# Last layer in groups of three token tiles, its outer weights converted there

## The chip, the cores and the metric

The kernel runs on one core of a Trainium2 chip. Its time is the device time of one execution in microseconds (us); lower is better. A core has a matrix engine (PE, with its own weight loads, PEld), a vector engine (DVE), a scalar engine (ACT), a general engine (POOL) and a queue engine (SP) that issues the transfers (DMA). Each works through its own list of instructions in order and waits on semaphores of the others. Products are summed in PSUM, eight banks of 2 KB in each of 128 partitions; everything else lies in SBUF.

## The reference

Attention with rotary positions (4 batches, 8 heads, 576 tokens, 64 wide), a soft mixture of 8 experts with 32 slots, and one more layer of 512 to 2048 to 512 with Mish in the middle. The last layer's weights arrive as float64.

```
attn  = softmax(rotate(q) @ rotate(k).T / 8) @ v              # x: 2304 x 512
logits = x @ phi                                              # 2304 x 32
slot_input = softmax(logits, over tokens).T @ x               # 32 x 512
slot_out[e] = relu(slot_input[e] @ w1[e]) @ w2[e]             # 8 experts, 4 slots each
x = softmax(logits, over slots) @ slot_out
h = x @ w_in                                                  # 512 x 2048, float64 given
g = h * tanh(log1p(exp(h)))
out = g @ w_out                                               # 2048 x 512, float64 given
```

## The kernel before

The attention goes through 16 pairs of heads; the table PLAN (lines 27 to 37) interleaves, row by row, the scores of one pair (S, M, E: products, maximum, exponential) with the transposes and products of the pair before (T, K, V, W, X), the rotation of the next, and steps of two side jobs: C is a step of the conversion, F one of the experts' dispatch. A scheduler then moves instructions within each engine's list.

The conversion (lines 492 to 531) turns float64 into float32 by the words of a number, 128 x 512 numbers at a time: load (cv_load, line 186's dma), two scalings on ACT (509, 510), three bit operations on DVE (519 to 521), a product and a sum on POOL (528, 529), and a store to DRAM (531). 32 of them run in the attention: the first 16 make w_in (scr_in), the other 16 make w_out (scr_out). Two raw buffers and two results alternate.

The experts follow: h_ps (line 800) over w1 and so_ps (816) over w2, whose 32 blocks of 1 MB come in through a ring of buffers (fetch, 120, used, 140); NRB = 7 of these are new when the attention has closed. so_ps gives s_t (827), the slots' outputs.

The last layer never forms x: for slices of 256 of the 2048 middle units `inner(j)` (871) multiplies s_t with w_in (m_wp), sums over four partition groups (m_w) and writes wst, and `combine(b)` (858) turns one batch's slot shares into ct, both as a high and a low part, so that wst x ct gives h. A unit is 256 tokens by 256 middle units: `mish(u)` makes hp, g in a high (gh) and a low part (gl); `second(u)`, four units later, adds twelve products (gh with wo_h and wo_l, gl with wo_h) to two sums o_ps. `outer(j)` (850) splits w_out, loaded from scr_out, into wo_h and wo_l. Units go by token tile: 9 tiles, 8 slices in each. PSUM: four banks for hp, two for inner until unit 8, then two more for sums.

## Time and profile before

| | |
|---|---|
| Time, median of 3 runs (lowest to highest) | 687.81 us (687.39 to 689.45) |
| The profiled execution | 682.22 us, its span 680.4 us |
| PE busy | 626.9 us (92%) |
| DVE busy | 399.3 us (59%) |
| ACT busy | 323.9 us (48%) |
| POOL busy | 251.2 us (37%) |
| DMA moved | 115.73 MB, mean 170 GB/s |

Busy shares are means over stages: the attention takes up to about 400 us, the experts up to about 440, the last layer the rest. A matrix engine that is shown as busy is not at its peak, since its ends are modelled. The chain that ended last is followed back from the last instruction, at each step to what released it. In the rows further down an engine's idle time stands with what ended it.

### The profile page before, as it was taken

What the parts mean: (1) busy time and instruction counts of PE and PEld (TensorE: products, weight loads), DVE (VectorE), ACT (ScalarE), POOL (GpSimd) and SP (SyncE); (2) the same over time, 40 slices, a digit from 0 to 9 for tenths busy, and PEclk for the clock granted to TensorE, in tenths of its full rate; (3) what the DMA queues carried; (4) which work ended last, traced back from release to release, by engine and by line L of the source; (5) the groups of instructions that cost most, each with busy time, mean ns of one, the idle gap of its engine ahead of it and who ended that gap; (6) DMA issues with size and microseconds to landing.
All of it is one profiled execution on the core that took longest, in us unless ns stands there. A gap on an engine that the chain in (4) does not pass through costs nothing.

```text
span 680.4 us, 11169 instructions
## 1 busy us (share of the span) xinstructions
PE 626.9 (92%) x4002; PEld 461.8 (68%) x4002; DVE 399.3 (59%) x819; ACT 323.9 (48%) x738; POOL 251.2 (37%) x287
## 2 busy tenths in 40 slices
PE   1698889989999989999999988989999999999997
PEld 1565566767667766776777662356888888888885
DVE  6678767896768877776866540066743343434330
ACT  3656756775767667766765510054412221221220
POOL 6668758866868675786330010000000000000000
PEclk9899989999999979999999999999999999999999
DMA  9777698989688975875577697990000110100111
GB/s 266 178 183 197 179 259 226 254 255 264 167 262 256 291 210 206 244 214 157 185 220 214 233 384 286 349 375 1 32 1 31 32 32 0 32 33 0 32 31 32
DMA packets 63064, 115.73 MB, mean 170 GB/s; under 512 B 13216, under 2 KB 25632, under 8 KB 62496
## 3 DMA queue, kind: packets, MB, share of 16 engines
q1 hardware_dynamic: 63008, 115.01, 55.8%
q8 instruction: 32, 0.52, 0.3%
q14 instruction: 24, 0.20, 0.1%
HBM read 73.40 MB, written 13.11 MB: 127 GB/s over the span
## 4 chain that ended last, share of the span: by engine, by line
PE 66%; DMA 10%; DVE 9%; ACT 6%; SPq 4%; issue 3%; POOL 1%; ACTq 0%; DVEq 0%; POOLq 0%
PE o_ps L923 29%; PE m_av L427 8%; PE t L372 5%; DMA w<-in_moe_w_in_dram 5%; PE s L331 4%; DMA qk_st<-partl 3%; PE s L333 3%; PE hp L899 3%; SPq L315 2%; PE h_ps L800 2%; PE so_ps L816 2%; DVE nmax L359 2%; ACT P L365 2%; DMA w<-in_moe_w_out_dram 2%; PE s L351 1%
## 5 line engine op out<-in xcount | busy, mean ns | idle before, releaser
L359 DVE TENSOR_REDUCE nmax<-s 128x1 f32<-128x576 f32 x144 | 107.9, 751 | 51.3 <-PE s L333 32.8
L365 ACT ACTIVATE P<-s,nmax 128x576 f32<-128x576 f32 x144 | 107.0, 744 | 21.4 <-DVE nmax L359 20.4
L923 PE MATMUL o_ps<-wo_l,gh 128*128 128x512 f32 x288 | 113.5, 395 | 0.0
L923 PE MATMUL o_ps<-wo_h,gh 128*128 128x512 f32 x288 | 111.8, 393 | 0.5 <-ACT wo_h L854 0.4
L923 PE MATMUL o_ps<-wo_h,gl 128*128 128x512 f32 x288 | 112.1, 390 | 0.0
L905 ACT ACTIVATE gg<-hp 128x512 f32<-128x512 f32 x72 | 43.1, 600 | 129.1 <-PE hp L899 110.7
L331 PE MATMUL s<-qk_st 128*128 128x288 f32 x256 | 86.5, 352 | 16.2 <-ACT P L365 6.3
L906 DVE CAST gh<-gg 128x512 fp32r<-128x512 f32 x72 | 30.6, 426 | 104.7 <-ACT gg L905 104.6
L372 PE MATMUL t<-cs,P 128*128 128x128 f32 x512 | 80.8, 286 | 8.9 <-DVE partl L271 5.9
L372 PEld LDWEIGHTS t<-cs,P 128*128 128x128 f32 x512 | 62.5, 146 | 20.2 <-issue 11.0
L331 PEld LDWEIGHTS s<-qk_st 128*128 128x128 f32 x256 | 50.0, 195 | 38.2 <-ACT P L365 13.2
L408 ACT COPY PT<-t 128x512 f32<-128x512 f32 x93 | 53.8, 585 | 43.8 <-PE t L372 42.8
L333 PE MATMUL s<-k_st,qk_st 128*128 128x288 f32 x256 | 74.2, 303 | 0.0
L427 PE MATMUL m_av<-PT,w 128*64 128x320 f32 (+1 forms) x384 | 70.1, 420 | 0.2 <-ACT PT L408 0.2
L923 PEld LDWEIGHTS o_ps<-wo_h,gl 128*128 128x128 f32 x288 | 54.1, 188 | 11.9 <-issue 0.4
L923 PEld LDWEIGHTS o_ps<-wo_l,gh 128*128 128x128 f32 x288 | 54.3, 189 | 10.1 <-DVE wo_l L855 1.1
L923 PEld LDWEIGHTS o_ps<-wo_h,gh 128*128 128x128 f32 x288 | 53.8, 188 | 10.4 <-ACT wo_h L854 1.1
L528 POOL TENSOR_TENSOR w<-w,w 128x512 f32<-128x512 f32 x32 | 41.8, 1305 | 39.8 <-ACT P L365 15.3
L229 POOL TENSOR_TENSOR w<-w,cs 128x512 f32<-128x512 f32 x34 | 45.6, 1344 | 22.8 <-PE m_k L283 11.9
L907 DVE TENSOR_TENSOR gl<-gg,gh 128x512 fp32r<-128x512 f32 x72 | 49.7, 692 | 6.6
L333 PEld LDWEIGHTS s<-k_st,qk_st 128*128 128x128 f32 x256 | 50.5, 197 | 0.0
L226 POOL TENSOR_TENSOR w<-w,cs 128x512 f32<-128x512 f32 x34 | 45.1, 1325 | 8.1 <-DMA w<-in_k_dram 4.4
(165 smaller groups left out, 995.3 us busy)
## 6 DMA issues: line engine op xcount, KB each, us to landing
w<-in_moe_w_dram SPq DMA_DIRECT2D x28, 1024.0 KB, 7.1
w<-in_moe_w_in_dram SPq DMA_DIRECT2D x16, 512.0 KB, 5.8
w<-in_moe_w_out_dram SPq DMA_DIRECT2D x16, 512.0 KB, 4.7
qk_st<-parth SPq DMA_DIRECT2D x46, 144.0 KB, 3.8
qk_st<-partl SPq DMA_DIRECT2D x46, 144.0 KB, 3.9
w<-in_q_dram SPq DMA_DIRECT2D x16, 256.0 KB, 5.4
w<-in_k_dram SPq DMA_DIRECT2D x16, 256.0 KB, 4.9
w<-in_moe_w_dram SPq DMA_DIRECT2D x16, 256.0 KB, 5.4
```

What stands on the lines that cost most here:

```text
L226: eng.tensor_tensor(out=tb, in0=src, in1=sin.to_broadcast([128, n, w]), op=ALU.mult)
L229: eng.tensor_tensor(out=dst, in0=sv, in1=cv, op=ALU.mult)
L331: nc.tensor.matmul(s[:, half, 0:288], lhsT=st[:, qc:qc + 128], rhs=st[:, KC + o:KC + o + 288], start=first, stop=False)
L333: nc.tensor.matmul(s[:, half, 0:288], lhsT=st[:, qc:qc + 128], rhs=k2_st[p % 2][:, o:o + 288], start=False, stop=last)
L359: nc.vector.tensor_reduce(out=stat[p][0][:, i:i + 1], in_=s[:, :, 0:288], axis=AX.XY, op=ALU.max, negate=True)
L365: nc.scalar.activation(out=P[p, t][:, h * S:(h + 1) * S].rearrange("p (a b) -> p a b", a=2), in_=s[:, :, 0:288], func=AF.Exp, bias=stat[p] ...
L372: nc.tensor.transpose(ps[:, j, :], P[p, t][:, blk * 128:(blk + 1) * 128], ident)
L408: nc.scalar.copy(dst, src)
L427: nc.tensor.matmul(ps[o:o + 64, :], lhsT=lhsT, rhs=rhs, start=(c == 0), stop=(c == 4))
L905: nc.scalar.activation(out=gg, in_=hp, func=AF.Mish)
L907: nc.vector.tensor_tensor(out=gl, in0=gg, in1=gh.bitcast(F32), op=ALU.subtract)
L923: nc.tensor.matmul(ps, lhsT=g_[:, cols], rhs=w_[f], start=(j == 0 and x == 0 and k_ == 0), stop=(j == NG - 1 and x == 1 and k_ == 2))
```

## The change

The conversion of w_out leaves the attention: PLAN loses five of its eleven C steps, scr_out is gone. The same words are now converted in the last layer from raw blocks that are loaded straight from w_out (load_out, four buffers), with the product and the sum on DVE, not POOL (low_word), and are split at once into wo_h and wo_l (outer). The four combine steps move into the second expert product; ct lies in a pool of its own there, and NRB falls from 7 to 6. Units now go in groups of three token tiles: for each slice three units, six sums in PSUM at a time, two banks left for hp and inner. In the first 24 units ACT makes gh. Two loads of ACT's function tables are placed by hand. Low parts of wst and ct change places among the partition groups.

```diff
-    "X0- R- C C S M E",
+    "X0- R- C S M E",
...
-    NRA, NRB, NRC = 8, 7, 3
+    NRA, NRB, NRC = 8, 6, 3
...
+    def scale_words(t):
+        lo, hi = words(t)
+        nc.scalar.activation(out=hi.bitcast(F32), in_=hi.bitcast(F32), func=AF.Copy, scale=2.0 ** -112)
+        nc.scalar.activation(out=lo.bitcast(F32), in_=lo, func=AF.Copy, scale=2.0 ** -52)
+
+    def high_word(t, sg, w):
+        hi = words(t)[1]
+        nc.vector.tensor_scalar(out=sg, in0=hi, scalar1=0x80000000, scalar2=None, op0=ALU.bitwise_and)
+        nc.vector.scalar_tensor_tensor(out=w, in0=hi, scalar=3, in1=sg, op0=ALU.logical_shift_left, op1=ALU.bitwise_or)
+        nc.vector.tensor_scalar(out=sg, in0=w, scalar1=0xFF800000, scalar2=None, op0=ALU.bitwise_and)
+
+    def low_word(eng, t, sg, w):
+        sg = sg.bitcast(F32)
+        eng.tensor_tensor(out=sg, in0=sg, in1=words(t)[0].bitcast(F32), op=ALU.mult)
+        eng.tensor_tensor(out=w, in0=w, in1=sg, op=ALU.add)
...
-        nc.sync.dma_start(out=scr_in[fb, :, c, :] if i < 16 else scr_out[i - 16], in_=w)
+        nc.sync.dma_start(out=scr_in[fb, :, c, :], in_=w)
...
-    steps = [lambda i=i, f=f: f(i) for i in range(NFB * KDM + NFC) for f in (cv_more, cv_act, cv_bits, cv_sum)]
+    steps = [lambda i=i, f=f: f(i) for i in range(NFB * KDM) for f in (cv_more, cv_act, cv_bits, cv_sum)]
...
+    tc.keep_in_program_order(nc.scalar.preload_act_table_set("mish"))
...
             for g in range(4):
                 used((2, 4 * eg + g, hf))
+            if 2 * eg + hf < 3:
+                for b in ((0,), (1, 2), (3,))[2 * eg + hf]:
+                    combine(b)
...
-    ps_p = ctx.enter_context(tc.tile_pool(name="ps_p", bufs=4, space=PSUM, reuse_waits="tile"))
-    ps_o = [ctx.enter_context(tc.tile_pool(name="ps_o", bufs=2, space=PSUM, reuse_waits="tile"))]
+    ps_p = ctx.enter_context(tc.tile_pool(name="ps_p", bufs=2, space=PSUM, reuse_waits="tile"))
+    ps_o = ctx.enter_context(tc.tile_pool(name="ps_o", bufs=6, space=PSUM, reuse_waits="tile"))
...
+    def load_out(c):
+        if c < NFC:
+            tc.keep_in_program_order(
+                nc.sync.dma_start(out=raws[c % 4], in_=w_out[c * 128:(c + 1) * 128, :].bitcast(U32)))
+
+    def outer(c):
+        t = raws[c % 4]
+        w = p6.tile([128, DM], F32, tag="w", name="w", bufs=2)
+        sg = p6.tile([128, DM], U32, tag="sg", name="sg", bufs=2)
+        scale_words(t)
+        high_word(t, sg, w.bitcast(U32))
+        low_word(nc.vector, t, sg, w)
+        nc.scalar.copy(wo_h[c], w)
+        nc.vector.tensor_tensor(out=wo_l[c], in0=w, in1=wo_h[c].bitcast(F32), op=ALU.subtract)
+
+    for x in (0, "i0", 1, 2, 3, "i1"):
+        if isinstance(x, int):
+            load_out(x)
+        else:
+            fetch((3, int(x[1]), 0), behind=True)
...
+    GR = 3
+    units = [(g * GR + i, j) for g in range(NU // GR) for j in range(NG) for i in range(GR)]
...
-        nc.vector.tensor_copy(gh, gg)
+        (nc.scalar.copy if u < NG * GR else nc.vector.tensor_copy)(gh, gg)
...
+    outer(0)
+    outer(1)
+    inner(0)
+    for u in range(len(units) + LOOK):
+        if u < len(units):
             mish(u)
+            g, j = units[u][0] // GR, units[u][1]
+            i = units[u][0] % GR
+            if g == 0:
+                if i < 2:
+                    load_out(2 * j + 4 + i)
+                if i == 0 and j % 2 == 0 and 2 + j // 2 < NFB:
+                    fetch((3, 2 + j // 2, 0), behind=True)
+                if j + 1 < NG:
+                    if i < 2:
+                        outer(2 * j + 2 + i)
+                    if i == 1:
+                        inner(j + 1)
         if u >= LOOK:
             second(u - LOOK)
```

Three places of the built order. The first is ACT in the attention, at the ninth pair of heads (P, z: the exponential of a score tile; w_4_0_97: the raw words under conversion). Before:

```order
L365 ACTIVATE P,z<-s,nmax 128x576
L399 COPY PT<-t4r 64x64
L267 CAST parth<-m_rem 128x2x2x64
L509 ACTIVATE w_4_0_97<-w_4_0_97 128x512
L510 ACTIVATE w_4_0_97<-w_4_0_97 128x512
L365 ACTIVATE P,z<-s,nmax 128x576
L288 ACTIVATE parth<-m_k 128x512
```

Now, at the same exponentials:

```order
L364 ACTIVATE P,z<-s,nmax 128x576
L398 COPY PT<-t4r 64x64
L266 CAST parth<-m_rem 128x2x2x64
L364 ACTIVATE P,z<-s,nmax 128x576
L287 ACTIVATE parth<-m_k 128x512
```

The scalings between the two exponentials are gone. Of before's 32 conversions the last stands behind 108 of the 144 exponentials; of the 16 that stay in the attention the last stands behind 58.

The second is PE where the last layer begins (m_sot: the slots' outputs turned, m_ct: combine, m_wp and m_w: inner). Before:

```order
L826 MATMUL m_sot<-cs,si_t 128x32 x4
L864 MATMUL m_ct<-cs,c_all 32x128 x20
L877 MATMUL m_wp<-w_0_0_4910,s_t 32x256 x4
L881 MATMUL m_w<-wp,cs 128x256
L877 MATMUL m_wp<-w_0_0_4910,s_t 32x256 x4
L899 MATMUL hp<-ct,wst 128x256 x2
L864 MATMUL m_ct<-cs,c_all 32x128 x20
L881 MATMUL m_w<-wp,cs 128x256
```

Now:

```order
L856 MATMUL m_sot<-cs,si_t 128x32 x4
L911 MATMUL m_wp<-w_0_0_4879,s_t 32x256 x4
L915 MATMUL m_w<-wp,cs 128x256
L932 MATMUL hp<-ct,wst 128x256 x4
L911 MATMUL m_wp<-w_0_0_4879,s_t 32x256 x4
L957 MATMUL o_ps<-wo_h_4843,gh 128x512
```

The combine products are no longer there; the first o_ps follows the second unit's hp and half of the second inner product.

The third is ACT at the same place (gg: Mish, wo_h: the rounded outer weights, raw: raw words of w_out). Before:

```order
L868 CAST ct<-m_ct 128x512
L868 CAST ct<-m_ct 128x64
L879 COPY wp<-m_wp 128x256
L883 CAST wst<-m_w 128x256
L879 COPY wp<-m_wp 128x256
L905 ACT_TABLE_LOAD
L905 ACTIVATE gg<-hp 128x512
```

Now:

```order
L497 ACTIVATE raw<-raw 128x512
L498 ACTIVATE raw<-raw 128x512
L896 CAST wo_h_4843<-w 128x512
L913 COPY wp<-m_wp 128x256
L497 ACTIVATE raw<-raw 128x512
L498 ACTIVATE raw<-raw 128x512
L497 ACTIVATE raw<-raw 128x512
L498 ACTIVATE raw<-raw 128x512
L917 CAST wst<-m_w 128x256
```

The copies wp and wst of the first inner product now stand behind the rounding of the first block and behind the scalings of the second and third.

## Rows read from the trace of the kernel before

**Rows 1.** The page: the span.

```profile
span 680.4 us, 11169 instructions
```

**Rows 2.** The page, its chain that ended last: shares of the span by line.

```profile
PE o_ps L923 29%; PE m_av L427 8%; PE t L372 5%; DMA w<-in_moe_w_in_dram 5%; PE s L331 4%; DMA qk_st<-partl 3%; PE s L333 3%; PE hp L899 3%; SPq L315 2%; PE h_ps L800 2%; PE so_ps L816 2%; DVE nmax L359 2%; ACT P L365 2%; DMA w<-in_moe_w_out_dram 2%; PE s L351 1%
```

**Rows 3.** Six stretches: length, busy us of PE, PEld, DVE, ACT, POOL; clock, DMA share, GB/s.

```profile
134.70:157.20 22.50, 19.17 (x129) 15.17 (x127) 18.04 (x43) 16.60 (x43) 14.35 (x16) 0.92 0.84 241
157.20:181.70 24.50, 24.26 (x169) 16.40 (x168) 18.97 (x39) 16.52 (x39) 17.66 (x19) 1.00 0.73 222
228.90:251.80 22.90, 19.92 (x130) 15.62 (x128) 17.91 (x44) 17.04 (x45) 14.67 (x17) 0.85 0.82 239
251.80:278.60 26.80, 26.70 (x184) 17.52 (x183) 19.24 (x41) 17.16 (x40) 18.47 (x21) 1.00 0.74 233
323.50:341.50 18.00, 18.00 (x134) 13.87 (x132) 14.34 (x39) 14.54 (x40) 6.85 (x11) 1.00 0.60 184
341.50:366.20 24.70, 24.70 (x185) 17.06 (x184) 15.01 (x33) 14.23 (x36) 3.97 (x8) 1.00 0.69 192
```

**Rows 4.** Groups of the conversion: busy us, mean ns | idle before, releaser.

```profile
L509 ACT ACTIVATE w<-w 128x512 f32<-128x512 f32 x32 | 21.9, 683 | 20.8 <-DMA w<-in_moe_w_in_dram 15.0 <-DMA w<-in_moe_w_out_dram 5.7
...
L519 DVE TENSOR_SCALAR w<-w 128x512 uint32<-128x512 uint32 x32 | 22.5, 702 | 1.3 <-POOL cvw L529 1.1
...
L528 POOL TENSOR_TENSOR w<-w,w 128x512 f32<-128x512 f32 x32 | 41.8, 1305 | 39.8 <-ACT P L365 15.3 <-issue 9.1 <-ACT w L510 7.0
```

**Rows 5.** The conversion's lines on DVE: ns min/median/max, first and last start in us.

```profile
L519 DVE TENSOR_SCALAR w<-w x32: 408/430/1486, 18.1 to 313.1; 128x512 uint32<-128x512 uint32 x32
...
L520 DVE SCALAR_TENSOR_TENSOR w<-w,w x16: 670/694/1460, 19.6 to 305.9; 128x512 uint32<-128x512 uint32 x16
...
L521 DVE TENSOR_SCALAR w<-w x16: 395/412/900, 21.2 to 307.6; 128x512 uint32<-128x512 uint32 x16
```

**Rows 6.** The chain in order of time: start us, length us, what.

```profile
425.14 13.99 PE so_ps L816 x128
...
451.43 1.93 PE o_ps L923 x6
...
492.33 2.76 PE o_ps L923 x12
...
662.21 13.64 PE o_ps L923 x60
```

**Rows 7.** Timeline where the last layer begins: start us, length us.

```profile
441.02 0.29 DVE L827 COPY s_t<-m_sot 128x128 f32<-128x128 f32 x1 [1.17 <-PE m_sot L826]
...
444.86 1.28 ACT L905 ACT_TABLE_LOAD   x1
```

**Rows 8.** Groups of the last layer: busy us, mean ns | idle before, releaser.

```profile
L907 DVE TENSOR_TENSOR gl<-gg,gh 128x512 fp32r<-128x512 f32 x72 | 49.7, 692 | 6.6
L905 ACT ACTIVATE gg<-hp 128x512 f32<-128x512 f32 x72 | 43.1, 600 | 129.1 <-PE hp L899 110.7 <-issue 18.3
...
L855 DVE TENSOR_TENSOR wo_l<-wo_l,wo_h 128x512 fp32r<-128x512 f32 x16 | 10.5, 685 | 0.1
L854 ACT CAST wo_h<-wo_l 128x512 fp32r<-128x512 f32 x16 | 9.1, 624 | 0.0
L885 DVE TENSOR_TENSOR wst<-m_w,wst 32x256 fp32r<-32x256 f32 x16 | 6.8, 424 | 4.5 <-ACT wst L883 4.3
...
L881 PE MATMUL m_w<-wp,cs 128*128 128x256 f32 x16 | 5.3, 411 | 1.2 <-ACT wp L879 1.0
...
L864 PE MATMUL m_ct<-cs,c_all 128*32 128x128 f32 x160 | 5.2, 275 | 0.0
L877 PE MATMUL m_wp<-w,s_t 128*32 128x256 f32 x64 | 5.1, 390 | 0.0
```

**Rows 9.** Line 136, the issue at 431.8 us, last of its weights: time to landing.

```profile
DMA to landing us min/median/max: 5.3/5.3/5.3
```

**Rows 10.** Stretch of the second expert product, columns as in rows 3.

```profile
425.00:441.00 16.00, 15.11 (x142) 5.11 (x144) 1.04 (x3) 0.37 (x2) 0.00 (x0) 1.00 0.94 345
```

More of the change, by code (lines that the diff above doesn't have):

```diff
@@ L525, in cv_sum @@
         t, sg, w = conv.pop(i)
-        lo = t.rearrange("p (n two) -> p n two", two=2)[:, :, 0].bitcast(F32)
-        sg = sg.bitcast(F32)
-        nc.gpsimd.tensor_tensor(out=sg, in0=sg, in1=lo, op=ALU.mult)
-        nc.gpsimd.tensor_tensor(out=w, in0=w, in1=sg, op=ALU.add)
-        fb, c = divmod(i % 16, KDM)
-        nc.sync.dma_start(out=scr_in[fb, :, c, :] if i < 16 else scr_out[i - 16], in_=w)
+        low_word(nc.gpsimd, t, sg, w)
+        fb, c = divmod(i, KDM)
+        nc.sync.dma_start(out=scr_in[fb, :, c, :], in_=w)
     dmat = {}
@@ L633, in filler @@
                 fill.pop(0)()
+    nc.scalar.preload_act_table_set("exp_and_friends")
     for i in range(2):
@@ L808, with combine @@
                 used((1, 4 * eg + g, hf))
+    tc.keep_in_program_order(nc.scalar.preload_act_table_set("mish"))
+    def combine(b):
+        for t0, nt in ((0, 4), (4, 1)):
+            ps = ps_m.tile([128, nt, 128], F32, tag="m", name="m_ct")
+            for j in range(nt):
+                for o in range(0, 128, 32):
+                    nc.tensor.matmul(ps[o:o + 32, j, :], lhsT=c_all[:, b, t0 + j], rhs=ident, start=True, stop=True)
+            n = 512 if nt == 4 else R
+            src = ps.rearrange("p t n -> p (t n)")[:, 0:n]
+            dst = ct[:, b * S + t0 * 128:b * S + t0 * 128 + n]
+            nc.scalar.copy(dst, src)
+            for o in (32, 96):
+                nc.vector.tensor_tensor(out=dst[o:o + 32], in0=src[o:o + 32], in1=dst[o:o + 32].bitcast(F32),
+                                        op=ALU.subtract)
     so_ps = ps_m.tile([128, DM], F32, tag="m", name="so_ps")
@@ L841 @@
     wst = p3.tile([128, F2], F32R, name="wst")
-    ct = p3.tile([128, NT], F32R, name="ct")
-    for c in range(NFC):
-        if c % 4 == 0:
-            fetch(take(*rooms.pop(0)), behind=True)
-        tc.keep_in_program_order(nc.sync.dma_start(out=wo_l[c].bitcast(F32), in_=scr_out[c]))
-    p6 = ctx.enter_context(tc.tile_pool(name="p6", bufs=6, reuse_waits="tile"))
-    def outer(j):
-        for c in (2 * j, 2 * j + 1):
-            raw_w = wo_l[c].bitcast(F32)
-            tc.keep_in_program_order(nc.scalar.copy(wo_h[c], raw_w))
-            nc.vector.tensor_tensor(
-                out=wo_l[c], in0=raw_w, in1=wo_h[c].bitcast(F32), op=ALU.subtract)
@@ L858, in combine @@
-    def combine(b):
-        for t0, nt in ((0, 4), (4, 1)):
-            ps = ps_p.tile([128, nt, 128], F32, tag="p", name="m_ct")
-            for j in range(nt):
-                for o in range(0, 128, 32):
-                    nc.tensor.matmul(ps[o:o + 32, j, :], lhsT=c_all[:, b, t0 + j], rhs=ident, start=True, stop=True)
-            n = 512 if nt == 4 else R
-            src = ps.rearrange("p t n -> p (t n)")[:, 0:n]
-            dst = ct[:, b * S + t0 * 128:b * S + t0 * 128 + n]
-            nc.scalar.copy(dst, src)
-            nc.vector.tensor_tensor(out=dst[64:128], in0=src[64:128], in1=dst[64:128].bitcast(F32), op=ALU.subtract)
+    p6 = ctx.enter_context(tc.tile_pool(name="p6", bufs=3, reuse_waits="tile"))
@@ new lines @@
+    raws = []
+    for i in range(4):
+        if i % 2:
+            t = rooms[i][0].tile([128, 2048], U32, tag=rooms[i][1], name="raw")
+            raws += [t[:, 0:1024], t[:, 1024:2048]]
+        else:
+            take(*rooms[i])
+    for i in range(2):
+        take(p3, f"wi{i}")
+    def load_out(c):
[11 more added lines that the diff above has]
+        nc.vector.tensor_tensor(out=wo_l[c], in0=w, in1=wo_h[c].bitcast(F32), op=ALU.subtract)
@@ L912, in second @@
     def second(u):
-        i, j = divmod(u, NG)
+        i, j = units[u]
         gh, gl = gs.pop(u)
@@ L946 @@
     LOOK = 4
-    for u in range(NU * NG + LOOK):
-        for b in {0: (0,), 1: (1,), 9: (2,), 11: (3,)}.get(u, ()):
-            combine(b)
-        if u < NG:
-            inner(u)
-        if u == NG:
-            ring.close()
-            first.close()
-            ps_o.append(ctx.enter_context(tc.tile_pool(name="ps_o2", bufs=2, space=PSUM, reuse_waits="tile")))
-        if u < NU * NG:
-            mish(u)
-        if 1 <= u < NG + 1:
-            outer(u - 1)
+    outer(0)
[3 more added lines that the diff above has]
+        if u < len(units):
+            mish(u)
+            g, j = units[u][0] // GR, units[u][1]
[10 more added lines that the diff above has]
+                        inner(j + 1)
         if u >= LOOK:
             second(u - LOOK)
+    ring.close()
 _INS = ["q", "k", "v", "moe_phi", "moe_w1", "moe_w2", "moe2_w_in", "moe2_w_out"]
```

47 lines of the change are left out of this document (18 added, 29 removed).

## The prediction

> **What bounds the kernel now.** The profiled execution took 682.2 us, 680.4 of them its span [rows 1]; the 1.8 us around it stay. I read the shares of the chain first. No engine holds the whole span. The last layer's second product (o_ps, line 923) is 29% of the chain, and the rest is spread thin: products and transposes of the attention, and two kinds of load that exist only for the conversion of the outer weights, 5% for moe_w_in and 2% for moe_w_out [rows 2]. So there are two regimes, and I read each by its own view.
>
> The attention, up to about 400 us, is bound by latency: PE, DVE, ACT and POOL hand each other small pieces. The stretches of rows 3 run from one start of line 351 to the next (that line runs once in each of the 16 pairs of heads, so a stretch is one pair). The first two, the next two and the last two stand at the same places of three successive batches; the first four hold conversions, the last two hold none, since the last conversion starts at 313.1 us [rows 5]. With conversions POOL is busy for 14 to 19 us of a stretch, without for 4 to 7. ACT, which works strictly in order, stood idle for 20.8 us in front of the conversion's first scaling because the raw block had not landed, 5.7 of it for w_out [rows 4]; exponentials queue behind it.
>
> The last layer is bound by PE. From 492.3 to 662.2 us the chain repeats one unit (256 tokens by 256 middle units): 169.88 us for 57 units, 2.98 us each [rows 6]. 72 units are 214.6 us. The eight inner products cost PE 5.3 + 5.1 = 10.4 us, the four combine steps 5.2 us [rows 8]. Together 230.2 us. The layer really runs from the moment s_t is written, 441.02 + 0.29 = 441.3 us [rows 7], to the end of the last product, 662.21 + 13.64 = 675.85 us [rows 6]: 234.5 us. So only 4.3 us of waits can be won there, whatever is grouped how.
>
> **What the grouping itself does: nothing.** 72 units, the same twelve products and two middle products in each; only their order and their PSUM banks differ. Six banks hold sums, two are left for the middle products, where there were four. A unit lasts 2.98 us and its bank is free after one Mish of 0.60 us [rows 8], so two suffice in steady state. At a change of group the first bank's sum is copied out while two more units run. I cost it at 0.
>
> **What leaves the attention.** Sixteen of 32 conversions: each two scalings on ACT (the first 0.68 us), three operations on DVE (the first 0.70 on average), two on POOL (the first 1.31) [rows 4], a load of 512 KB, a store of 256 KB. They leave SP's in-order queue too, where q and k loads stand behind the stores. They do not thin out evenly. In the built order the 32nd conversion stood on ACT after twelve pairs' worth of exponentials; now the 16th stands after 6.4. So pairs 0 to 6 keep the density that they had, and about 5.4 pairs lose their conversions whole. The price of that is in rows 3: against the mean of its two counterparts the fifth stretch is shorter by 22.7 - 18.0 = 4.7 us, the sixth by 25.65 - 24.7 = 0.95 us. That is 2.8 us a pair. Part of the first difference is not the conversion: the fifth stretch also lacks the rotation of a next batch's remainder, four POOL operations. I take 2.2 us a pair, 5.4 x 2.2 = **12 us gained**. Bounds: 0.95 a pair gives 5 us, and if the first pairs don't keep even that, 4; 3.5 a pair (both stretches against the slower batch) gives 19.
>
> **What the last layer takes up.** Four parts, in the clock of before.
>
> Combine moves ahead. Its 5.2 us of PE [rows 8] now stand inside the second expert product, which ran from 425.14 for 13.99 us without a break [rows 6], so s_t comes 5.2 us later, at 446.5 us. The last weights of that product landed at 431.8 + 5.3 = 437.1 us [rows 9], under a DMA busy at 0.94 [rows 10]. One buffer of 1 MB fewer delays them by some 3 us (1 MB at the 345 GB/s of rows 10). That hides under the combine steps. In turn the last layer loses 5.2 us of PE. These two cancel: 0.
>
> The first accumulation comes later after s_t. Before, it came at 451.43 [rows 6], 10.1 us after s_t, with a combine step and three inner products in between. Now it waits for two blocks made from float64. Their raw buffers come free with the third quarter of the expert product, about 439.5 us; a load under a full queue took some 5 us [rows 9], so 444 to 445. A block is then two scalings (1.37), three bit operations (0.43 + 0.69 + 0.41) [rows 5], a product and a sum (0.69 each, the length of line 855), a rounding (0.62) and a difference (0.69) [rows 8]: 5.6 us in a row, and the second follows 3.6 us behind on DVE. That is 453 to 454 us; ACT, in order, has the copies of the first inner product behind the first rounding. So some 7 to 9 us after s_t, in which PE has only 2.6 us of work: 5 to 6 us of waits. The table load of 1.28 us that stood there [rows 7] is gone, worth 0.4.
>
> DVE then nearly keeps pace. It has 16 blocks of 0.43 + 0.69 + 0.41 + 3 x 0.685 = 3.59 us, 57.4 in all, 24 differences gl of 0.692, 16.6, and 8 for wst of 0.424, 3.4: 77.4 us [rows 5, 8]. PE has 24 x 2.98 + 10.4 = 81.9 us for the same units. At 94% in-order DVE will be late in the first units, until PE's own work gives it a lead: I add 3 to 4 us.
>
> Loads: 12 MB instead of 8 during these units. That is 35 us at 345 GB/s against 82: hidden.
>
> So waits go from 4.3 to about 10 us: **6 us lost**. Bounds: -1 (waits fall to 3, as DMA and DVE arrive in time) to 17 (below).
>
> Here a rule speaks against the change. DVE is the engine that fills up, POOL is empty from 441 us on, and yet two operations a block move from POOL to DVE. The Trainium skill, Perfetto Trace Analysis, section Optimizing Scalar/DVE Operations, says that when DVE is saturated offloading to ScalarE or even GPSIMD may make sense, though the two share a port. By that rule DVE is the pacer: the rival below. And of the port: line 519 took 0.43 us in the median but up to 1.49 in the attention [rows 5]. The Trainium skill, SBUF — State Buffer, section Who interferes with whom, says that DVE operations with two SBUF inputs, or in a two-port mode, contend with GpSimd reads. With POOL idle the medians should hold in the last layer; at line 519's mean of 0.70 instead [rows 4] a block would cost 3.86.
>
> **The sum.** 682.2 - 12 + 6 = 676.2 us for an execution like the profiled one. The median of the runs, 687.81, lies 5.6 above it; the same difference on the median gives **682 us**.
>
> **Rivals.**
> Slower, DVE paces: a block goes to and fro between DVE and ACT, both in order, and each wrong turn costs an idle gap. PE needs block 15 for unit 21; after it 51 units remain, 152 us. DVE starts at about 445 us and without a gap is through at 522, before PE asks, at 446.5 + 8 + 21 x 2.98 + 10.4 = 527.5. With gaps of X in all, and X above 6, the products end at 522 + X + 152 = 674 + X instead of 675.85: X - 2 lost. Against the 12 us gained it turns the sign at X = 14, and X = 20, a gap of a quarter, gives 694 us. For it: the 94%, and the order on ACT, where copies that PE waits for stand behind scalings. Against it: DVE may work four raw buffers ahead, and while PE waits DVE catches up.
> Slower, mild: the conversions were in gaps anyway. The sixth stretch, hardly shorter than its counterparts [rows 3], speaks for it, the fifth against. Gain 4, loss 6 to 7: 690.
> Even: gain and loss within 2 us of each other: 688.
> Larger gain: 3.5 us a pair, and the start of the layer finds its blocks ready: 19 - 3: 672.
>
> **Chances.** Forecast (679 to 685.7): 0.42; larger gain: 0.22; even: 0.15; conversions in gaps: 0.12; DVE paces: 0.09. The range 671 to 692 takes in all but DVE as pacer and the far end of the large gain. 0.3% (2 us) is about what a measurement of this kernel can tell from no change: faster 0.64, same 0.15, slower 0.21.
>
> **What would show it.** Right: pairs 7 to 11 take 2 to 3 us less each, pairs 0 to 6 about as long as now; ACT's wait for w_out before its scaling is gone; the expert product lasts 19 us instead of 14; the first o_ps comes 7 to 9 us after s_t; units settle at 2.98 us by the fifth or so. Wrong: waits of PE on wo_l or gl through all 24 units (DVE paces), pairs 7 to 11 as long as now, or waits on hp's two banks.

## The result

| | before | after |
|---|---|---|
| Median, us (lowest to highest) | 687.6 (685.7 to 689.5), 4 runs | 680.1 (677.7 to 682.4), 4 runs |
| Ratio after / before | | 0.989, 95% interval 0.9845 to 0.9936 |
| The profiled execution, us | 682.2 | 679.2 |

The new kernel is 7.5 us faster; 5.8 were forecast. A second measurement gave 680.9 against 688.2, ratio 0.9898 (0.9862 to 0.9935). The two profiled executions are only 3.0 us apart. Where the other 4.5 us are is a question for the experiments.

The page of after: its span, and the shares of the chain by line. The load of w_out in the attention, 2% in [rows 2], is gone; what stands here under that name is the raw blocks of the last layer.

```profile
span 677.3 us, 11071 instructions
...
PE o_ps L957 28%; PE m_av L426 14%; PE t L371 8%; PE s L330 5%; PE s L332 4%; PE s L350 3%; DMA w<-in_moe_w_in_dram 3%; PE hp L932 2%; PE so_ps L843 2%; DMA raw<-in_moe_w_out_dram 2%; PE m_lg L452 2%; SPq L185 1%; DMA w<-in_moe_w_dram 1%; PE tk L385 1%; ACT P L364 1%
```

**The attention of after.** The same six pairs as in [rows 3], cut at the same line (now 350): length, busy us of PE, PEld, DVE, ACT, POOL with counts; clock, DMA share, GB/s.

```profile
132.20:155.40 23.20, 19.25 (x128) 14.95 (x126) 18.39 (x42) 14.74 (x37) 12.57 (x15) 0.90 0.71 209
155.40:184.50 29.10, 27.64 (x189) 18.55 (x187) 19.75 (x40) 17.01 (x42) 17.21 (x18) 0.96 0.67 182
226.10:243.40 17.30, 17.30 (x130) 13.63 (x128) 13.76 (x39) 13.68 (x38) 5.15 (x9) 1.00 0.53 147
243.40:268.10 24.70, 24.70 (x184) 17.07 (x183) 14.90 (x32) 14.52 (x37) 12.54 (x17) 1.00 0.68 183
311.60:329.30 17.70, 17.34 (x124) 12.88 (x122) 12.81 (x37) 11.75 (x33) 3.16 (x7) 1.00 0.30 94
329.30:357.70 28.40, 28.40 (x198) 19.02 (x197) 16.64 (x35) 15.73 (x37) 6.00 (x10) 1.00 0.71 193
```

The third and fourth have lost their conversions: 22.9 and 26.8 us have become 17.3 and 24.7, and PE is busy in all of them. The second and sixth are longer than before because the cut now holds more of PE's work (189 products instead of 169, 198 instead of 184). So single pairs mislead, and sums over many pairs are read instead. One row for pairs 1 to 6 and one for 7 to 15, first of before, then of after, same columns:

```profile
40.40:181.70 141.30, 127.83 (x866) 92.55 (x866) 107.45 (x215) 96.08 (x227) 104.20 (x114) 0.98 0.80 223
181.70:386.60 204.90, 198.70 (x1373) 141.90 (x1370) 147.13 (x322) 137.69 (x333) 117.30 (x142) 0.98 0.75 227
```

```profile
41.70:184.50 142.80, 131.14 (x879) 93.07 (x879) 106.43 (x215) 92.87 (x223) 101.57 (x111) 0.98 0.75 211
184.50:377.90 193.40, 193.04 (x1359) 138.55 (x1357) 121.08 (x279) 120.02 (x299) 75.61 (x112) 1.00 0.64 181
```

Pairs 7 to 15 lost 11.5 us. Pairs 1 to 6 are 1.5 us longer, and PE idles in them 142.8 - 131.1 = 11.7 us, in the others 0.4. Of the 16 conversions 12 lie in pairs 1 to 6; before, 13 lay there and 16 in pairs 7 to 12 (by the starts of POOL's last sum). The groups that answer to [rows 4] (busy us, mean ns | idle before, releaser):

```profile
L503 DVE TENSOR_SCALAR w<-w 128x512 uint32<-128x512 uint32 x16 | 12.3, 770 | 3.0 <-ACT w L497 2.0 <-issue 0.8
...
L497 ACT ACTIVATE w<-w 128x512 f32<-128x512 f32 x16 | 10.8, 673 | 5.7 <-DMA w<-in_moe_w_in_dram 5.7
```

ACT's wait ahead of the attention's scalings fell from 20.8 to 5.7 us, all of it for w_in now. The first bit operation takes 0.77 us in the mean here, where POOL works beside it.

**The last layer of after.** The chain in order of time (start us, length us, what): the first hp, the first sums, a raw block that ACT waited for, the last products.

```profile
444.62 0.81 PE hp L932 x2
...
447.19 4.78 PE o_ps L957 x12
...
480.81 3.22 DMA raw<-in_moe_w_out_dram
...
659.03 13.64 PE o_ps L957 x60
```

The timeline of its start, first ACT, then DVE, then PE; in brackets the idle time before, and what ended it.

```profile
440.13 0.62 ACT L896 CAST wo_h<-w 128x512 fp32r<-128x512 f32 x1 [5.61 <-DVE w L510]
440.65 0.36 ACT L913 COPY wp<-m_wp 128x256 f32<-128x256 f32 x1
...
443.16 0.38 ACT L917 CAST wst<-m_w 128x256 fp32r<-128x256 f32 x1
```

```profile
436.58 0.29 DVE L857 COPY s_t<-m_sot 128x128 f32<-128x128 f32 x1 [1.23 <-PE m_sot L856]
436.90 0.43 DVE L503 TENSOR_SCALAR sg<-raw 128x512 uint32<-128x512 uint32 x1
```

```profile
438.14 1.08 PE L911 MATMUL m_wp<-w,s_t 128*32 128x256 f32 x8 [1.59 <-DVE w L504]
441.07 1.22 PE L915 MATMUL m_w<-wp,cs 128*128 128x256 f32 x2 [1.85 <-ACT wp L913]
444.62 1.22 PE L932 MATMUL hp<-ct,wst 128*128 128x256 f32 x4 [2.33 <-DVE wst L918]
...
447.12 0.80 PE L957 MATMUL o_ps<-wo_h,gh 128*128 128x512 f32 x1
...
448.14 0.63 PE L957 MATMUL o_ps<-wo_h,gh 128*128 128x512 f32 x1
...
451.10 0.40 PE L957 MATMUL o_ps<-wo_h,gh 128*128 128x512 f32 x1
```

s_t is written at 436.87 us, and the first o_ps comes 10.25 us after it. The copy wp was ready to go when m_wp ended, but stood on ACT behind the rounding of block 0, which waited 5.61 us for DVE; wst stood behind the scalings of blocks 1 and 2. Block 0 itself was not late to land: ACT had scaled it by 434.52 us, but its first bit operation starts at 436.90, right behind the copy of s_t in DVE's list; whether it could have gone ahead of that copy was not tried. The products up to 451 us take 0.63 instead of 0.40 us. The stretch view shows the clock beside them, and the share of DVE in the first 65 us; columns as above:

```profile
436.90:447.10 10.20, 4.52 (x22) 1.87 (x22) 9.00 (x18) 6.17 (x13) 0.00 (x0) 0.53 0.96 393
447.10:451.10 4.00, 4.00 (x13) 3.15 (x10) 4.00 (x9) 2.96 (x6) 0.00 (x0) 0.50 0.71 240
436.90:501.90 65.00, 58.53 (x286) 43.70 (x287) 62.62 (x117) 47.55 (x92) 0.00 (x0) 0.89 0.46 166
```

In the 10.2 us in which PE was busy for 4.5 its granted clock was 0.53 of full, so mostly at the lower of its two levels (1.2 of 2.4 GHz), and it stayed at 0.50 for the first 4 us of o_ps; DVE was busy 62.6 of 65 us. From its first o_ps to its last PE waits 0.8 us in all, for gh: none of the waits that the prediction named as signs of being wrong (on wo_l, on gl, on hp's two banks) is there. From s_t to the end of the last product (672.67) the layer takes 235.8 us, before 234.5 [rows 6, 7].

### The profile page after: what moved, and what is told of

It reads as the page before. It is cut to its first block, busy times and chain, and to the rows that moved or that the text cites. A ratio compares the mean times of both kernels' runs of the same rounds, so it can differ in the third digit from the quotient of the medians.

```text
span 677.3 us, 11071 instructions
## 1 busy us (share of the span) xinstructions
PE 626.2 (92%) x4002; PEld 461.1 (68%) x4002; DVE 404.9 (60%) x833; ACT 332.7 (49%) x755; POOL 206.8 (31%) x255
## 4 chain that ended last, share of the span: by engine, by line
PE 77%; DMA 7%; DVE 5%; ACT 5%; SPq 2%; issue 2%; POOL 2%; ACTq 0%; DVEq 0%; POOLq 0%
PE o_ps L957 28%; PE m_av L426 14%; PE t L371 8%; PE s L330 5%; PE s L332 4%; PE s L350 3%; DMA w<-in_moe_w_in_dram 3%; PE hp L932 2%; PE so_ps L843 2%; DMA raw<-in_moe_w_out_dram 2%; PE m_lg L452 2%; SPq L185 1%; DMA w<-in_moe_w_dram 1%; PE tk L385 1%; ACT P L364 1%
## 5 line engine op out<-in xcount | busy, mean ns | idle before, releaser
L957 PE MATMUL o_ps<-wo_h,gh 128*128 128x512 f32 x288 | 114.9, 399 | 0.8 <-ACT gh L940 0.8
L957 PE MATMUL o_ps<-wo_h,gl 128*128 128x512 f32 x288 | 108.4, 391 | 0.0
L371 PEld LDWEIGHTS t<-cs,P 128*128 128x128 f32 x512 | 59.9, 144 | 23.1 <-issue 11.6
L426 PE MATMUL m_av<-PT,w 128*64 128x320 f32 (+1 forms) x384 | 73.1, 421 | 0.9 <-ACT PT L396 0.6
L330 PEld LDWEIGHTS s<-qk_st 128*128 128x128 f32 x256 | 49.7, 194 | 31.0 <-ACT P L364 11.5
L940 DVE CAST gh<-gg 128x512 fp32r<-128x512 f32 x48 | 20.5, 427 | 75.0 <-ACT gg L938 75.0
L957 PEld LDWEIGHTS o_ps<-wo_h,gl 128*128 128x128 f32 x288 | 54.2, 188 | 11.7 <-DVE sg L509 0.4
L426 PEld LDWEIGHTS m_av<-PT,w 128*64 128x64 f32 x384 | 26.6, 136 | 22.2 <-issue 9.0
```

The lines of the kernel that those rows point to most:

```text
L330: nc.tensor.matmul(s[:, half, 0:288], lhsT=st[:, qc:qc + 128], rhs=st[:, KC + o:KC + o + 288], start=first, stop=False)
L371: nc.tensor.transpose(ps[:, j, :], P[p, t][:, blk * 128:(blk + 1) * 128], ident)
L426: nc.tensor.matmul(ps[o:o + 64, :], lhsT=lhsT, rhs=rhs, start=(c == 0), stop=(c == 4))
L957: nc.tensor.matmul(ps, lhsT=g_[:, cols], rhs=w_[f], start=(j == 0 and x == 0 and k_ == 0), stop=(j == NG - 1 and x == 1 and k_ == 2))
```

## Experiments

Times are medians, each against runs of the kernel before on the same chip. "The layer" is the time from s_t to the end of the last product in the profile.

### The attention alone, the last layer alone, the words alone

```diff
-        tc.keep_in_program_order(nc.sync.dma_start(out=wo_l[c].bitcast(F32), in_=scr_out[c]))
+        tc.keep_in_program_order(nc.sync.dma_start(out=wo_l[c].bitcast(F32), in_=scr_in[c // 4, :, c % 4, :]))
```

(on the kernel before, with the new PLAN and 16 conversions)

> The kernel before, with the new kernel's table PLAN and without the 16 conversions of w_out; experts and last layer stay as they were. The outer blocks are read from the converted blocks of w_in instead (same size, same place in the queue), so the output is not the layer's. Theory (the gain sits in the attention, the loss at the start of the last layer): the attention gives all of its gain and nothing is taken back. The two profiles differ by 8.7 us up to the start of the experts, so 687.6 - 9 = 678 to 679 us, and with the 12 to 13 us that the two medians would need (7.5 gained in all, 5 to 6 lost at the end) 675. The last layer lasts 234 to 235 us from s_t to the last product, with its first o_ps 10 us after s_t, as in the kernel before. Rival (the gain comes from the last layer's groups or from the combine steps inside the expert product): within 2 us of the kernel before, 686 to 690.

Measured: 676.5 against 688.9 us, ratio 0.984 (0.9792 to 0.9888): **12.4 us less**. The layer takes 235.0 us, its first o_ps 10.2 us after s_t, as before. The gain is the attention's.

```diff
-        w = p6.tile([128, DM], F32, tag="w", name="w", bufs=2)
-        sg = p6.tile([128, DM], U32, tag="sg", name="sg", bufs=2)
-        scale_words(t)
-        high_word(t, sg, w.bitcast(U32))
-        low_word(nc.vector, t, sg, w)
+        w = t[:, 0:DM].bitcast(F32)
```

(on the new kernel, with the kernel before's PLAN, 32 conversions, and blocks loaded from scr_out)

> The new kernel's experts and last layer (groups of three, six sums, combine in the expert product), but w_out is converted in the attention by the kernel before's PLAN, all 32 conversions; outer then only rounds and subtracts. Computes everything. Theory (grouping costs and gives nothing, the combine move cancels): 687.6, within 2 us either way. s_t comes 18 to 19 us after the first so_ps instead of 16, the layer from s_t to the last product takes 229 to 231 us (230.2 less the 5.2 of combine, plus 4 to 6 of waits). Rival (the grouping itself gains): 680 to 683, and the whole difference between the two kernels would be here. Rival (two banks for the middle products are too few): 690 or more, with PE's waits on hp spread over all 72 units.

Measured: 690.5 against 688.9 us, ratio 1.0022 (0.9981 to 1.0062): **no difference**, +1.5. In its profile s_t came 20.7 us after the first so_ps, in the kernel before 16.2; the layer took 231.5 us, 3.0 less. The first o_ps came 6.4 us after s_t.

The third run has the same five lines left out of the new kernel, with blocks of 512 KB from w1.

> The new kernel with the word conversion in the last layer left out: two scalings, three bit operations, product and sum of each of 16 blocks. The blocks are loaded with the same 512 KB each, but from w1, and rounded and subtracted as they are, so the output is not the layer's. Theory (the 10.8 us of waits come mostly from the conversion: the first inner product's copies stand on ACT behind block 0 and the scalings of 1 and 2, and PE's clock falls while it waits): first o_ps 6 to 7 us after s_t instead of 10.25, waits 5 to 7 us, time 4 to 6 us below the new kernel's 680.1: 674 to 676. Rival (the start is bound by the landing of the first block of w_in and by the chain of inner, the conversion hides behind it): 679 to 680. Rival (DVE at 94 per cent holds PE back through all 24 units): more than 8 us below, under 672.

Measured: 677.5 against 688.9 us, ratio 0.9862 (0.9815 to 0.9909), so 11.4 less; the layer took 232.7 us, 3.1 less than with the words where 4 to 6 were expected, and the first o_ps came 8.15 us after s_t, not 6 to 7. DVE is busy 24 of the first 65 us there. So the three parts are -12.4 for the attention, +1.5 for groups, combine and the smaller changes that come with them, and for the words in the layer 3.1 (by the layer) to 3.9 us (by the medians, -11.4 against -7.5). They add up to -7.8 to -7.0; the whole change measured -7.5 and -7.3.

### POOL does the low words

```diff
-        low_word(nc.vector, t, sg, w)
+        low_word(nc.gpsimd, t, sg, w)
```

> The new kernel with the product and the sum of each block of the last layer on POOL instead of DVE, as the attention has them. Computes everything. POOL takes 1.3 us for each of the two where DVE takes 0.69, so a block's chain is 1.2 us longer, while DVE's work for the first 24 units falls from 77 to 55 us. Theory (only the first blocks' chain counts, DVE is not the pacer afterwards): 0 to 3 us slower, 680 to 683, first o_ps 10 to 12 us after s_t, DVE's other operations as long as now. Rival (a nearly full DVE holds PE back): faster by 2 us or more, 678 or less, and no second stall near 45 us after s_t. Rival (POOL's operations lengthen those of DVE that run beside them): line 503's median above 0.43 us, time above 683.

Measured: 703.9 against 688.9 us, ratio 1.0232 (1.0172 to 1.0291): some **23 us slower than the new kernel**, the layer 256.9 us. By its time that was the third case, and far beyond its size; the first o_ps came 9.3 us after s_t, so the loss is not at the start. Groups of this run from 440 to 540 us (busy us, mean ns | idle before):

```profile
L510 POOL TENSOR_TENSOR w<-w,sg 128x512 f32<-128x512 f32 x16 | 24.6, 1540 | 1.3
...
L941 DVE TENSOR_TENSOR gl<-gg,gh 128x512 fp32r<-128x512 f32 x20 | 21.7, 1110 | 5.8 <-ACT gh L940 5.8
L504 DVE SCALAR_TENSOR_TENSOR w<-raw,sg 128x512 uint32<-128x512 uint32 x16 | 19.3, 1205 | 0.5
...
L503 DVE TENSOR_SCALAR sg<-raw 128x512 uint32<-128x512 uint32 x16 | 11.6, 722 | 1.5 <-ACT raw L497 1.4
...
L918 DVE TENSOR_TENSOR wst<-m_w,wst 64x256 fp32r<-64x256 f32 x7 | 3.0, 428 | 8.2 <-ACT wst L917 8.1
```

The same groups of the new kernel in its last layer, POOL idle:

```profile
L941 DVE TENSOR_TENSOR gl<-gg,gh 128x512 fp32r<-128x512 f32 x72 | 49.4, 690 | 8.9 <-ACT gh L940 4.4
...
L504 DVE SCALAR_TENSOR_TENSOR w<-raw,sg 128x512 uint32<-128x512 uint32 x16 | 11.0, 686 | 0.1
...
L503 DVE TENSOR_SCALAR sg<-raw 128x512 uint32<-128x512 uint32 x16 | 6.8, 423 | 0.2 <-ACT raw L497 0.2
...
L918 DVE TENSOR_TENSOR wst<-m_w,wst 64x256 fp32r<-64x256 f32 x8 | 3.4, 427 | 8.8 <-ACT wst L917 8.7
```

With POOL at work beside them, the three DVE operations shown that work on SBUF alone take 1.6 to 1.76 times as long in the mean; wst, which reads one operand from PSUM, is unchanged. The means mix two kinds. Line 503 in the layer of this run, ns min/median/max:

```profile
L503 DVE TENSOR_SCALAR sg<-raw x16: 412/422/1523, 440.7 to 507.7; 128x512 uint32<-128x512 uint32 x16
```

Its median is unchanged, against what the third case had said, and single operations take up to 1.52 us: some keep their length, others are held up by as much as 1.1 us, within the 1.3 to 1.7 us of one POOL operation. Two operations a block left DVE (1.37 us), but the rest grew by more: DVE was busy 62.5 of the first 65 us, as in the new kernel, and did 72 operations in them instead of 117, of which some 32 were of the two kinds that moved. The Trainium skill, SBUF — State Buffer, section Who interferes with whom, has DVE and GpSimd share a port pair as a lock that one holds for a whole instruction; these rows agree.

### The same programs once more

> The new kernel once more, unchanged, on the chip of the three that follow, for a second profile. Theory (the profiles of one program differ in the stretch where conversions run, and nowhere else): pairs 7 to 15 take 193.4 us as in the first profile, within 0.2; s_t to the last product 235.8, within 0.5; pairs 1 to 6 (142.8 us in the first profile) up to 4 us off. Time 678 to 682. Rival (executions differ everywhere): pairs 7 to 15 or the last layer off by over 1 us.

> The kernel before once more, unchanged, for a second profile of it. Theory (its first profile, 682.2 us, was a short execution, and the difference lies in the stretch with conversions): pairs 7 to 15 within 2 us of 204.9 (conversions run in 7 to 12), pairs 1 to 6 longer than 141.3 by 2 to 5 us, s_t to the last product 234.5 within 0.5, time of the profiled execution 684 to 690. Rival (the executions differ in the last layer or the experts): 234.5 or the 33.4 us from the first h_ps to s_t off by over 1 us.

Measured: after 680.9 us (8 runs, 679.9 to 683.9), before 687.5 (10 runs, 684.8 to 690.7). Pairs 1 to 6 and 7 to 15 of the second profile of after, then of before, columns as above:

```profile
42.20:185.80 143.60, 132.39 (x882) 94.69 (x880) 106.24 (x216) 93.23 (x223) 101.45 (x111) 0.96 0.75 209
185.80:379.90 194.10, 193.23 (x1359) 138.51 (x1357) 121.08 (x279) 120.34 (x299) 75.60 (x112) 1.00 0.64 181
```

```profile
41.60:182.60 141.00, 128.06 (x867) 92.10 (x866) 106.73 (x215) 95.84 (x227) 104.70 (x114) 0.98 0.80 222
182.60:390.30 207.70, 197.84 (x1373) 141.32 (x1371) 145.99 (x322) 137.27 (x333) 117.54 (x142) 0.99 0.75 224
```

The layer repeats to 0.1 us (235.8 and 235.9; 234.5 and 234.5). Stretches full of conversions do not: pairs 7 to 15 of before 204.9, 207.7, and 206.8 in the run with the last layer alone, which has the same 32 conversions; pairs 1 to 6 of the three took 141.3, 141.0 and 144.2. Pairs 1 to 6 of the new attention ran from 142.8 to 146.4 us in seven profiles, its pairs 7 to 15 only from 193.4 to 194.1 (I had allowed 0.2). My expectation had put the difference of before's two profiles in pairs 1 to 6; it was in 7 to 15. Before's first profile, 682.2 us, lay below each of its four timed runs (685.7 to 689.5), so it was a short one, which explains 3.0 against 7.5.

### An earlier start of the last layer

```diff
-    outer(0)
+    outer(0, lambda: inner(0))
+    scale_words(raws[1])
+    mish(0)
+    mish(1)
+    with tc.issue_after(last[0]):
+        scale_words(raws[2])
+        scale_words(raws[3])
     outer(1)
-    inner(0)
```

(with the copies of inner(0), and Mish and gh of units 0 and 1, held in this order on ACT)

> The new kernel with another order on ACT at the start of the last layer: the two copies of the first inner product, and Mish and rounding of the first two units, no longer stand behind block 0's rounding and the scalings of blocks 1 to 3. Computes everything. Theory (PE waits there for copies that are queued behind other work on ACT): hp comes 2 to 3 us earlier, first o_ps 6.5 to 8 us after s_t instead of 10.25, 2 to 3.5 us faster than the new kernel: 677 to 678. Rival (the blocks of w_out are what is late, then): first o_ps earlier, but PE waits as long for blocks 1 to 3 afterwards, time 680 to 681, no gain. Rival (the landing of the first block of w_in sets everything): first o_ps still 10 us after s_t.

```diff
+    wps = ps_o.tile([128, 128], F32, tag="o", name="warm")
+    def hold(n):
+        for _ in range(n):
+            tc.keep_in_program_order(nc.tensor.matmul(wps, lhsT=ident, rhs=ident, start=True, stop=True))
```

(7 ahead of m_wp, 8 ahead of m_w, 9 ahead of hp; the copy wp held behind the rounding of block 0)

> The new kernel with 24 products of the identity with itself (128 x 128, result unused) in PE's gaps between the turned slot outputs, the first inner product's two steps and the first hp, ACT's order there kept. Computes everything. Theory (PE's clock falls to half because it stands idle between 436 and 447 us, and that costs some 2 us: ten o_ps at 0.63 instead of 0.40 us, two small products twice as long): granted clock of the stretch from s_t to 15 us after it above 0.9 instead of 0.5 to 0.6, first o_ps 0.5 to 1 us earlier, 1.5 to 2.5 us faster than the new kernel: 678. Rival (the clock falls for another reason than idleness): granted clock still 0.5, no gain. Rival (the waits are for others anyway, a faster PE only waits longer): clock up, time 680 to 681.

Measured, on the chip that gave the new kernel 680.9: 684.6 for the first and 683.8 us for the second, so **both about 3 us slower**. The ranges of the runs overlap (682.8 to 688.8 and 679.2 to 687.2, against 679.9 to 683.9), but the layer, which repeats to 0.1 us, took 239.3 and 239.0 us instead of 235.9. The start did improve in the first: first o_ps 7.24 us after s_t. In the second the granted clock was 1.00 for the first 10 us after s_t, but then fell to 0.50 for some 3 us, just as o_ps began: eight of the first o_ps took 0.63 to 0.69 us there as well, and the clock over 15 us was 0.89, not above 0.9. So the fall was put off, and this run doesn't test its price. The waits of PE later on, in the first (444 to 470 us; us in total, times, longest), are 4.4 us, where the new kernel, from its first o_ps to 470 us, waits 0.6:

```profile
PE hp L943 <- ACT raw L498: 2.0, 1, 2.0
PE hp L943 <- DVE wst L928: 1.3, 1, 1.3
PE o_ps L968 <- ACT gh L951: 1.1, 1, 1.1
```

In both, the scheduler had also reordered ACT's later work: the wst of the third and fourth slice comes 1.7 and 4.6 us later after s_t in the first run, and in the second ACT's order differs from 11 us after s_t on. Whether the loss is that order or DVE's load could not be told here; the last two runs take it up.

### The conversions spread out

```diff
-        scale_words(conv[i])
+        hi = words(conv[i])[1]
+        tc.keep_in_program_order(nc.scalar.activation(
+            out=hi.bitcast(F32), in_=hi.bitcast(F32), func=AF.Copy, scale=2.0 ** -112))
+        lo = words(conv[i])[0]
+        nc.scalar.activation(out=lo.bitcast(F32), in_=lo, func=AF.Copy, scale=2.0 ** -52)
```

> The new kernel with each conversion's first scaling held behind the ACT instruction that stands ahead of it in the program, so that the 16 conversions go through some eleven pairs of heads as PLAN has them (the last one behind 93 exponentials instead of 58). Computes everything. Theory (a conversion costs time only where it is dense: in the two profiles PE idles 11.7 us in pairs 1 to 6, and not at all in pairs 7 to 12, where DVE is busy 12.7 us of 21.8): pairs 1 to 6 lose 3 to 6 us, pairs 7 to 11 gain at most 2, time 675 to 678. Rival (each conversion costs its 0.7 us or so wherever it stands, since ACT and DVE are in order): pairs 1 to 6 shorter by as much as pairs 7 to 11 get longer, time 679 to 682. Rival (the pins themselves hold ACT up, as each scaling then waits for its load in front of exponentials): slower, over 683.

Measured: **669.9 us** against 688.2, ratio 0.9751 (0.9712 to 0.9791), and against 680.9 of the new kernel on the same chip: 11.1 us less, where I had expected 3 to 6. Its pairs 1 to 6 and 7 to 15:

```profile
41.50:174.60 133.10, 127.52 (x881) 90.45 (x879) 98.87 (x204) 88.56 (x214) 92.13 (x105) 1.00 0.76 204
174.60:368.10 193.50, 190.13 (x1359) 139.20 (x1357) 129.60 (x296) 127.48 (x312) 89.88 (x122) 0.99 0.71 200
```

Six of the 16 conversions now lie in pairs 7 to 10 (POOL's last sum starts at 258.6 us instead of 188.9), and pairs 7 to 15 take 193.5 us as with hardly any: there they are free. Pairs 1 to 6, with nine instead of twelve, are 9.7 us shorter: PE idles 5.6 us there instead of 11.7, and is busy for 3.6 us less with as many products, at a granted clock of 1.00 instead of 0.98. The layer is unchanged, 236.0 us.

That could be the hold and not the density. So the same hold, with the conversions close together by the kernel before's PLAN:

```diff
-    "X0- R- C S M E",
+    "X0- R- C C S M E",
```

(and the four other steps)

> The kernel of the run before this one (conversions held to their place in the program, 669.9 us), with the kernel before's table PLAN, eleven conversion steps a pair in place of six: the 16 conversions are through after 52 exponentials, instead of 93 there and 58 in the new kernel. Computes everything. Theory (density is what costs): the early gain is lost, pairs 1 to 6 take 140 us or more instead of 133, time 678 to 684, as the new kernel. Rival (the hold itself orders ACT better, wherever the conversions are): 668 to 672. Between them both count.

Measured: 682.9 against 688.6 us, ratio 0.9925 (0.9898 to 0.9953). The gain is gone; 15 of the 16 conversions lie in pairs 1 to 6, held as firmly as in the run before:

```profile
37.30:186.00 148.70, 131.52 (x882) 92.55 (x880) 106.08 (x217) 96.34 (x229) 111.28 (x120) 0.97 0.80 221
186.00:382.70 196.70, 196.34 (x1359) 139.38 (x1357) 121.86 (x280) 119.38 (x297) 70.72 (x107) 1.00 0.59 169
```

So the hold alone is not the gain. Density and place are less well told apart. In the later pairs density counts: six conversions in pairs 7 to 10, 1.5 a pair, cost nothing, while before's 16 in pairs 7 to 12, 2.7 a pair, made pairs 7 to 15 longer by 11.5 to 13.6 us. In pairs 1 to 6 nine, twelve and fifteen conversions go with 133.1, 142.8 to 146.4 and 148.7 us; a fixed price of some 3 us for each conversion in just these pairs is not excluded, since no run has fewer than nine there. Nor does a run separate what a conversion costs on the engines from what its load and store cost. Pairs 7 to 15, with no conversion in them, take 196.7 us here and at most 194.1 in the new kernel; why stays open.

### Spread, with the start of the layer in a fixed order

ACT's first 24 units follow a list (S scaling, H rounding of a block; P, W the copies of inner; G, R Mish and gh of a unit). The issues of the later loads move with it, each behind the sum of the block whose buffer it refills.

```diff
+FIRST = (
+    "S0 P0 S1 W0 H0 G0 R0 G1 R1 H1 S2 P1 S3 W1 H2 S4 G2 R2 S5 H3 "
...
```

> The spread conversions of the kernel at 669.9 us, and ACT's whole order in the first 24 units of the last layer held as written: the first inner product's copies and the first two units' Mish and rounding ahead, the scalings of blocks 2 and 3 after them, from block 4 on about as the new kernel has them, so that no later copy falls behind as it did when only the start was reordered. Computes everything. Theory (the start can be had if the order behind it stays): first o_ps 7 to 8 us after s_t, no gap of over 1 us later, s_t to the end 233 to 234 us instead of 235.9, time 667 to 669. Rival (DVE has no slack in the first 60 us, so an earlier start only waits later): first o_ps earlier, s_t to the end still 235 to 237, time 669 to 671. Rival (a fixed order on ACT is worse than the scheduler's): over 237, time 672 or more.

Measured: 672.2 us, ratio 0.9765 (0.9735 to 0.9796). First o_ps 7.5 us after s_t, the layer 239.2 us: the third case. The two longest sums of PE's waits from 434 to 462 us:

```profile
PE hp L954 <- DVE wst L941: 2.7, 2, 2.0
PE hp L954 <- ACT gg L960: 1.2, 1, 1.2
```

The last run has the warm products of above, and the scheduler's own order of the spread kernel as its list: "S0 H0 P0 S1 S2 W0 S3 G0 G1 R0 H1 ...".

> The spread conversions of the kernel at 669.9 us, with 24 products of the identity with itself (result unused) in PE's gaps at the start of the last layer, and ACT's order there held word for word as that kernel has it; in the warm run before, ACT's order had moved from the fifth block on. Computes everything. Theory (the half clock by itself costs about what the ten slow o_ps show, 0.2 us each, and holding ACT's order keeps that gain): granted clock from s_t to 15 us after it above 0.9, s_t to the last product 233.5 to 235.5 us instead of 236.0, time 667.5 to 669.5. Rival (what PE wins early it waits for later, since DVE is full for the first 65 us): s_t to the last product within 0.5 of 236.0, time 669 to 671. Rival (a PE that runs ahead meets later copies, as in the three kernels with an earlier start): 238 or more, time 672 or more.

Measured: 669.5 us, ratio 0.9756 (0.9691 to 0.9821). The first 10.2 us after s_t, 3.1 us soon after them, and the first 65 us, columns as above; then one of the o_ps from the second stretch:

```profile
426.70:436.90 10.20, 7.99 (x69) 6.34 (x67) 8.72 (x18) 6.13 (x13) 0.00 (x0) 1.00 0.78 308
437.30:440.40 3.10, 3.10 (x9) 2.35 (x8) 3.10 (x7) 2.71 (x6) 0.00 (x0) 0.50 1.03 412
426.70:491.70 65.00, 60.81 (x329) 46.94 (x327) 61.78 (x117) 47.60 (x91) 0.00 (x0) 0.97 0.47 169
```

```profile
437.80 0.63 PE L1000 MATMUL o_ps<-wo_h,gh 128*128 128x512 f32 x1
```

ACT's order was the same, and the layer took 236.8 us against 236.0: nothing won, nearly the second case. But this is no test of the half clock. The clock was full only for the 10.2 us in which PE had little to do for the layer; then it fell to 0.50, although PE had been busy for 8.0 of these 10.2 us, and nine of the first o_ps took 0.51 to 0.63 us, as eight do in the kernel at 669.9 us. Over the 15 us that the expectation named it was 0.89, not above 0.9. What the half clock costs in the end was therefore not measured. From the distance of the starts (0.43 us at half, 0.23 at full clock) nine slow o_ps take some 1.8 us longer; that is an estimate of their length, not of what their end would gain. Why the clock fell there stays open too.

PE waits 2.0 us for gh in the 25 us after the start, where the kernel at 669.9 us waits 0.6, and DVE is busy 61.8 of 65 us, 62.5 there. DVE's order changes 10.5 us after s_t. With ACT's order kept the layer is 0.8 us longer than without the warm products, in the first warm run 3.1, so most of that run's loss goes with ACT's order. For the two kernels with an earlier first inner product that is likely but not shown: what PE waits for in them is ACT as much as DVE.

## Why the prediction held, and where it did not

Right, 680.1 for 682.0, and for its main reason: the attention's gain (12 forecast, 12.4 measured) less what the experts and the layer lose (6 forecast, 4.6 to 5.4 measured).

**The attention, 12 us: right in size.** 12.4 alone. But the working took a price of 2.2 us a pair from [rows 3], as if each conversion that leaves saved its share. The spread run shows that no one price holds: six conversions in four later pairs cost nothing, and nine instead of twelve in pairs 1 to 6 save 9.7 us. Whether that is the number or the even spacing within a pair the runs don't separate; the hold alone, with 15 of them there, saves nothing. That 2.2 a pair, taken from two stretches of 4.7 and 0.95 us, came out so well is partly luck. The change won because it emptied pairs 7 to 12, where 16 stood. The step "pairs 0 to 6 keep the density that they had" was right, and was the hint I did not follow: the density there is the scheduler's, not PLAN's (held to PLAN's place, the 16th stands behind 93 exponentials instead of 58).

**"Pairs 7 to 11 take 2 to 3 us less each"** can't be read singly, as shown; over pairs 7 to 15 it is 11.5 us in the first pair of profiles and 13.6 in the second.

**Grouping and combine, 0: right.** +1.5, within the interval of none; s_t 4.5 us later for 5.2 predicted, so_ps over 18 us for 19. Units follow each other at 2.98 us only from about the 32nd on, not from the fifth, though PE hardly waits in between.

**The layer's waits, 4.3 to 10 us: right in sum (10.8), wrong in their parts.** After: 235.8 - (230.2 - 5.2) = 10.8. The first o_ps came after 10.25 us, not 7 to 9. I had the blocks late; what was late was the inner product, whose copies stand on ACT behind block 0's rounding. I mentioned that order and did not cost it; 5.7 us of idle PE came of it and of the chain around it. The 3 to 4 us for DVE in the first units came out at under 1 us of waits after the first o_ps. The half clock, which I had not named, took their place: PE's work up to the first o_ps took 4.5 us instead of 2.6, and the slow o_ps some 1.8 more (the estimate above). So the sum fits because two errors cancel, which is luck. What a full clock there would have saved no run shows.

**DVE as the pacer, 0.09: rightly small, but close.** Its operations took what [rows 5, 8] gave, and it was busy 96% of the first 65 us. After the first o_ps PE did not wait for it as things stood. In the two kernels that started PE earlier it waited for ACT (3.1 and 1.9 us) as well as for DVE (1.3 and 2.7). Without the words (DVE 24 of 65 us) the layer is 3.1 us shorter, no more.

**The rule on offloading** that I set against the change does not hold here: putting the two operations back on POOL costs 23 us.

**The step from 682.2 to the median.** I carried the difference of one profiled execution over to the median. Executions of before range over 8 us (683.5 to 691.5 in 13 runs on one chip), so that step had an error of some us; it happened to be small.

## To carry to other kernels

A side job in the gaps of a latency-bound stage need not have one price per piece: here six conversions at 1.5 a pair were free in the later pairs, and 16 at 2.7 a pair there cost 11.5 to 13.6 us. So look where the scheduler really puts it, and hold it to its place before moving it elsewhere; here one pin on 16 instructions was worth 11 us, more than the whole change. Before winning time at the start of a stage, see what PE will wait for in the next tens of microseconds: the two kernels that brought its first products 3 us forward lost more than that behind them. When a run is to test the clock, read the granted clock beside the products that were slow, not only before them. Two engines that slow each other are not two engines: sum their work with the lengthened durations.
